# RWKV attention into a Sinkhorn mixture of experts on one core: attention scores in two diagonal blocks of 64 tokens with a half state, and three moves in the start phase

## The chip, the core and the metric

The kernel runs on one core of a Trainium2 chip. The core has five engines that run side by side, each through its own list of instructions in order: TensorE (PE, matmuls; its weight loads are listed as PEld), VectorE (DVE), ScalarE (ACT), GpSimd (POOL) and SyncE (SP, which here issues the DMAs). An engine waits for another through semaphores that stand in its instructions. The matmuls write PSUM, eight banks of accumulators that DVE and ACT can read. The metric is the device time of one execution in microseconds, given as the median of several runs.

## The reference

The first half is a linear attention with a decaying state, token by token; the second half routes every token through eight experts, with gates balanced by eight Sinkhorn rounds.

```python
for t in range(S):                       # B=4, H=8, S=768, D=48
    kt, vt, rt = (k[:, :, t], v[:, :, t], r[:, :, t])
    cur = np.einsum('bhd,bhe->bhde', u[None] * kt, vt)
    y[:, :, t] = np.einsum('bhd,bhde->bhe', rt, state + cur)
    state = w[None, :, :, None] * state + np.einsum('bhd,bhe->bhde', kt, vt)
...
x = y.transpose(0, 2, 1, 3).reshape(B * S, H * D)        # 3072 x 384
P = np.exp(logits - logits.max())                        # logits = x @ w_gate
for _ in range(8):
    P /= P.sum(1, keepdims=True) + 1e-09
    P /= P.sum(0, keepdims=True) + 1e-09
    P *= N / E
for e in range(E):                                       # E=8, F=1024
    out += P[:, e:e + 1] * (np.maximum(x @ w1[e], 0.0) @ w2[e])
```

## The kernel before

**Tokens.** The 3072 tokens are 24 tiles of 128 (`NTT`), six tiles to a batch (`NCHB`). The attention is computed in chunks of 128 tokens: r and k are multiplied with tables of powers of the decay, so that within a chunk the scores of a head are one masked product, and what earlier chunks left is a state matrix per head. Heads lie in pairs (`NPAIR` = 4), one head of a pair on partitions 0 to 63, the other on 64 to 127.

**The steps.** A Python loop over `i` from 0 to `NTT + 2` writes the program in a software pipeline; step `i` writes, in this order: the loads of a later tile on SP; `prep(i+2)` (r on POOL, k on DVE, tiles `rp` and `kp`); `bonus_dot(i+1)` (POOL); `stage_b(i+1)` (PE transposes into `prT`, `pkT`, ACT copies to `rT`, `kT`); `scale_x` and `low_x` of tile `i-2` (DVE and ACT, tile `xsc`, then a transposing DMA to `hbx`); one unit of expert work on PE; `stage_c(i)`; up to two units of expert work; `stage_d(i-1)` and `finish(i-1)` (DVE or ACT make `x`); small gate products (`px`). Nothing reorders it afterwards: each engine runs its part in the order written, and a tile framework puts in the semaphore waits that the uses of the tiles ask for.

**Scores and state.** `stage_c` (line 473) makes the scores `pA` of a tile in two PSUM tiles, one for each half of the head pairs' partitions, in 16 matmuls of 64 by 64 weights over 128 columns. Two masked copies on DVE (`copy_predicated`) take them to `at`. The product k by v of the chunk, `pu`, goes to a PSUM tile of its own in 8 matmuls over all 128 tokens, unless the tile is the last of its batch, and DVE adds it to the state `S`, which POOL then multiplies with the decay of a chunk (`wbd`). In a batch's first tile the DVE does that multiplication itself.

**Output.** `stage_d` (line 518) makes `py`: 8 matmuls of the state (`py<-S`; none in a batch's first tile) and 16 of the masked scores (`py<-vn,at`).

**PSUM.** `prT`, `pkT`, the two `pA`, `pu` and `py` take turns in four buffers (pool `ps3`); a tile that takes a buffer waits until the one before it there has been read.

**Expert work beside it.** Tile by tile the finished `x` feeds the first expert: units of 9 matmuls (`ph<-hbx,ws`, then `hb` on ACT and DVE) and of 12 (`po<-ws,hb`, then `stg`). In steps 2 to 9 a plan (`PLAN`, line 696) places the splitting of that expert's weights into two f16 parts: maxima (`am`, `bm`), their reduction on DVE (`ar`, `br`), over partitions by PE (`ax`, `bx`), scales, high parts on ACT, low parts on DVE (`al`, `bl`). From step 9 on, further steps of DVE, ACT and POOL that combine tokens for the later experts are placed at two points of each step (`prepare`; `ws<-hbx` and `xv<-ws,xv` in the trace).

**After the attention** (line 813 on) come the other seven experts in 14 half stages, dense matmuls.

Of the kernel before, what the change touches and what calls it, by code (L numbers as in the profile page):

```python
# [8 lines left out]
F32 = mybir.dt.float32  # L9
# [4 lines left out]
ALU = mybir.AluOpType  # L14
# [19 lines left out]
def rwkv_sinkhorn_moe(  # L34
# [30 lines left out]
    HP = 64  # L65
# [5 lines left out]
    NSUM = 4  # L71
# [222 lines left out]
    def spin(n):  # L294
        pz = ps2.tile([P, TB], F32, tag="po", name="pz")
        for _ in range(n):
            T.matmul(pz, zeros[:, :P], zeros, start=True, stop=True)


    loads = {}  # L300
    early_home = xv0.rearrange("p n l q -> p (n l q)")

    def load_part(tt, nm, src):
        b, c = divmod(tt, NCHB)
        if 3 <= tt <= 5 and nm != "v":
            t_ = part(early_home, F32, (2 * (tt - 3) + "rk".index(nm)) * H * D, (H, D))
        else:
            t_ = ld.tile([P, H, D], F32, tag=nm + "n", name=f"{nm}n_{tt}", bufs=5 if nm == "v" else 3)
        Q.dma_start(t_, src[b, :, c * C : (c + 1) * C, :].rearrange("h t d -> t h d"))
        loads.setdefault(tt, {})[nm] = t_  # L310
# [38 lines left out]
            unit[:, :1, 1:].broadcast_to([P, n // HP, HP]), 0.0,  # L349
        )  # L350

    spin(13)
    wbd = ac.tile([P, NPAIR, 2, D], F32, name="wbd")
    mask = ac.tile([P, C], F32, name="mask")
    maski = mask.bitcast(I32)

    rp_ = [ac.tile([P, H, HP], F32, name=f"rp{i}") for i in range(2)]
    kp_ = [ac.tile([P, H, HP], F32, name=f"kp{i}") for i in range(3)]
    at_ = [ac.tile([P, H, C], F32, name=f"at{i}") for i in range(2)]

    ss_ = [ac.tile([P, NPAIR, 2, D], F32, name=f"S{i}") for i in range(3)]
    for t_ in rp_[:1] + kp_[:1] + rp_[1:] + kp_[1:]:
        G.memset(t_[:, :, D:], 0.0)
    fill(at_[0].rearrange("p h c -> p (h c)"))
# [25 lines left out]
    for j in range(2):  # L390
        rows = slice(j * HP, j * HP + D)
# [3 lines left out]
    for src, dst in ((tab, rtab), (tabr, ktab)):  # L395
# [6 lines left out]
    S_.copy(ub.rearrange("p h d -> p (h d)"), pub[:, : H * D])  # L402

    G.memset(mask, 1.0)
    G.affine_select(
        out=mask, in_=mask, compare_op=ALU.is_gt, fill=0.0, base=0,
        pattern=[[1, C]], channel_multiplier=-1,
    )
    for t_ in ss_:
        for j in range(2):  # L410
            G.memset(t_[j * HP : (j + 1) * HP, :, 1 - j, :], 0.0)

# [23 lines left out]
    st = {}  # L436
# [4 lines left out]
    def prep(tt):  # L441
        ld_ = loads[tt]
        (G if tt else V).tensor_tensor(rp_[tt % 2][:, :, :D], ld_["r"], rt4, op=ALU.mult)
        V.tensor_tensor(kp_[tt % 3][:, :, :D], ld_["k"], kt4, op=ALU.mult)
        st[tt] = {}

    def bonus_dot(tt):
        ld_ = loads[tt]
        rk = at2.tile([P, H, D], F32, tag="rk", name=f"rk_{tt}", bufs=3)
        G.tensor_tensor(rk, ld_["r"], ld_["k"], op=ALU.mult)  # L450
        G.tensor_tensor(rk, rk, ub, op=ALU.mult)
        st[tt]["rk"] = rk

    def bonus(tt):
        vn = loads[tt]["v"]
# [6 lines left out]
    def stage_b(tt):  # L462
        d = st[tt]
        for nm, src in (("rT", rp_[tt % 2]), ("kT", kp_[tt % 3])):
            pt = ps3.tile([P, NPAIR, P], F32, tag="pa", name=f"p{nm}_{tt}")
            sv = src.rearrange("p (a j) d -> p a (j d)", j=2)
            for p_ in range(NPAIR):
                T.transpose(pt[:, p_, :], sv[:, p_, :], ident)
            dst = at2.tile([P, NPAIR, P], F32, tag=nm, name=f"{nm}_{tt}", bufs=3 if nm == "rT" else 2)
            S_.copy(dst, pt)  # L470
            d[nm] = dst

    def stage_c(tt, between):
        d = st[tt]
        c = tt % NCHB
        rT, kT = d["rT"], d["kT"]
        at = at_[tt % 2].rearrange("p (a g) c -> p g a c", g=2)
        pas = []
        for g in range(2):
            pa = ps3.tile([P, NPAIR, C], F32, tag="pa", name=f"pA_{tt}_{g}")  # L480
            pas.append(pa)
        for a in range(NPAIR):
            for g in range(2):
                rows = slice(g * HP, g * HP + HP)
                for hs in (slice(0, HP), slice(HP, C)):
                    T.matmul(pas[g][hs, a, :], kT[rows, a, hs], rT[rows, a, :], start=True, stop=True)
        between()
        for g in range(2):
            V.copy_predicated(
                at[:, g], maski.unsqueeze(1).broadcast_to([P, NPAIR, C]), pas[g]  # L490
            )
        if c < NCHB - 1:
            vn = loads[tt]["v"]
            kp = kp_[tt % 3].rearrange("p (a j) d -> p a (j d)", j=2)
# [9 lines left out]
            for j in range(2):  # L504
                rows = slice(j * HP, (j + 1) * HP)
                if c == 0:
                    V.tensor_tensor(sn[rows, :, j, :], pu[rows], wbd[rows, :, j, :], op=ALU.mult)
                else:
                    V.tensor_tensor(sn[rows, :, j, :], pu[rows], d["S"][rows, :, j, :], op=ALU.add)
            if c:  # L510
                for j in range(2):
                    rows = slice(j * HP, (j + 1) * HP)
                    G.tensor_tensor(
                        sn[rows, :, j, :], sn[rows, :, j, :], wbd[rows, :, j, :], op=ALU.mult
                    )
            st.setdefault(("S", tt + 1), sn)

    def stage_d(tt):
        d = st[tt]
        c = tt % NCHB  # L520
# [5 lines left out]
        halves = [slice(i * HP, (i + 1) * HP) for i in range(2)]  # L526
        first = True
        pyf = py.rearrange("p h d -> p (h d)")
        if c > 0:
            for p_ in range(NPAIR):  # L530
                for hs in halves:
                    T.matmul(
                        pyp[hs, p_, :], d["rT"][:, p_, hs], d["S"][:, p_].rearrange("p j d -> p (j d)"),
                        start=first, stop=False, skip_group_check=True,
                    )
                first = False
        for h in range(H):
            for hs in halves:
                T.matmul(
                    py[hs, h, :], at[:, h, hs], vn[:, h, :],  # L540
                    start=first, stop=(h == H - 1 and tt >= NSUM), skip_group_check=True,
                )
            first = False
        d["py"] = pyf

    def finish(tt):
# [144 lines left out]
    for sg in range(3):  # L691
# [15 lines left out]
    def planned(i, pos):  # L707
        for nm in PLAN.get(i, {}).get(pos, "").split():
            wsteps.pop(nm)()
# [3 lines left out]
        3: [(7, "v")],  # L713
    }

    def n_steps(i, j):
# [8 lines left out]
    bonus_dot(0)  # L725
    for i in range(NTT + 3):
        if i == 1:
            gate_max()
        if i + 2 < NTT:
            for tt, nms in LOADS.get(i, [(i + 4, "rkv")]):  # L730
                for nm in nms if tt < NTT else "":
                    load_part(tt, nm, {"r": r, "k": k, "v": v}[nm])
            if i:
                prep(i + 2)
        if i + 1 < NTT and i:
# [26 lines left out]
        if i in (2, 3, 5):  # L762
            low_x(i - 2)
        if i == 4:
            for c_ in (slice(0, FHC), slice(FHC, FC)):
                Q.dma_start(raws[1][:, c_], w2[0, c_.start * P : c_.stop * P].rearrange("(c p) d -> p c d", p=P))
        planned(i, "b")
        if i == 0:
            fill(at_[1].rearrange("p h c -> p (h c)"))
            stage_b(1)  # L770
            bonus_dot(1)
            bonus(0)
        elif 5 <= i <= NTT:
            work(2 if i > 8 else 1)
# [603 lines left out]
```

## Time and profile before

| what | value |
|---|---|
| median of 3 runs | 1525.42 us (1524.48 to 1527.28) |
| the profiled execution's own time | 1524.22 us |
| its span, first to last instruction | 1522.7 us |
| PE matmul busy | 1508.2 us, 10280 records |
| DVE, ACT, POOL busy | 1000.7, 685.0, 568.8 us |
| attention, steps 0 to 24 | about the first 220 us |

A row of the timeline gives the start and the length of a run of equal instructions in us, the engine, the line, the operation with the tile that it writes and those that it reads, the shapes, the count, and in brackets how long the engine stood idle before and who ended that. Every line number there is 30, the helper through which all engines are called, so the tile names tell the places. An f32 matmul of the program leaves two records, so the 16 matmuls of the scores are `x32`. The end of a matmul's record is modelled and lies some hundred ns behind the start of the next one's; steps on PE are best read from start to start.

### The profile page before, as it was taken

Reading aid. Unit: us, or ns where it says so; the run is one execution under the profiler, and the core shown is the slowest. Engines: PE = TensorE matmul, PEld = TensorE weight load, DVE = VectorE, ACT = ScalarE, POOL = GpSimd, SP = SyncE. Lnnn points to the kernel's source line nnn. Section 1 sums busy time; section 2 is a strip of 40 time slices with the busy share of each in tenths; the row PEclk is TensorE's granted clock in tenths of the full one; section 3 lists DMA queues with packets and bytes.
Section 4 is the critical chain, followed back from the end, with each engine's and each line's share of the span. In section 5 each row is a group of like instructions: output and inputs, shape, how many; then the busy total and the mean of one; then the engine's idle time right before and its main releaser. Section 6 shows DMA issues by size and latency. Waiting matters only on the chain.

```text
span 1522.7 us, 26106 instructions
## 1 busy us (share of the span) xinstructions
PE 1508.2 (99%) x10280; PEld 852.8 (56%) x10280; DVE 1000.7 (66%) x1658; ACT 685.0 (45%) x1261; POOL 568.8 (37%) x682
## 2 busy tenths in 40 slices
PE   8999999999999999999999999999999999999998
PEld 6677765555555555555555555555555555555555
DVE  8877758676566666666676666666565666566563
ACT  6544434444354544545454544544354444444320
POOL 8677956010214234242524234242424233242200
PEclk9999999999999999999999999999999999999999
DMA  9655523211345676666656676645455454555434
GB/s 194 137 122 108 104 64 103 84 40 58 102 83 75 91 130 87 120 87 123 94 75 123 91 130 88 118 62 94 61 88 64 60 99 58 97 61 94 57 94 131
DMA packets 186725, 142.97 MB, mean 94 GB/s; under 512 B 109538, under 2 KB 180836, under 8 KB 186596
## 3 DMA queue, kind: packets, MB, share of 16 engines
q0 software_dynamic: 44928, 61.36, 32.5%
q1 hardware_dynamic: 141458, 79.87, 19.7%
q8 instruction: 82, 1.34, 0.4%
q14 instruction: 47, 0.39, 0.1%
q10 hardware_dynamic: 210, 0.00, 0.0%
HBM read 55.20 MB, written 80.23 MB: 89 GB/s over the span
## 4 chain that ended last, share of the span: by engine, by line
PE 95%; DVE 3%; ACT 1%; issue 1%; DMA 0%; ACTq 0%; DVEq 0%
PE po L30 49%; PE bZ L30 12%; PE bY L30 12%; PE ph L30 5%; PE bA L30 5%; PE bB L30 5%; PE bC L30 2%; PE py L30 2%; PE pA L30 1%; PE pu L30 1%; PE prT L30 1%; PE pkT L30 1%; DVE hb L30 0%; DVE at L30 0%; PE pz L30 0%
## 5 line engine op out<-in xcount | busy, mean ns | idle before, releaser
L30 PE MATMUL po<-ws,hbx 128*128 128x384 f16 x3360 | 736.8, 326 | 0.0
L30 POOL DMA_DIRECT2D accd<-stg x288 | 249.7, 867 | 694.9 <-ACT stg L30 674.3
L30 PEld LDWEIGHTS <-hbx 128*128 128x128 f16 x3504 | 334.1, 98 | 293.1 <-issue 0.6
L30 PEld LDWEIGHTS <-ws 128*128 128x128 f16 x3096 | 301.6, 98 | 247.1 <-DMA hbx<-xsc 2.5
L30 ACT ACTIVATE hbx<-tb 128x512 f16<-128x512 f32 x224 | 141.1, 630 | 448.6 <-DVE tb L30 448.6
L30 PE MATMUL po<-ws,hb 128*128 128x384 f16 x1248 | 323.0, 326 | 0.5 <-DVE ws L30 0.5
L30 DVE TENSOR_TENSOR tb<-bY,tb 128x512 f32<-128x512 f32 x168 | 116.1, 691 | 195.7 <-PE bY L30 195.4
L30 ACT ACTIVATE stg<-po,pe 128x384 f32<-128x384 f32 x312 | 179.2, 574 | 122.4 <-PE po L30 96.8
L30 PE MATMUL bZ<-xv,ws 128*128 128x512 f16 x840 | 227.0, 379 | 0.5 <-DVE tb L30 0.5
L30 PE MATMUL bY<-xv,ws 128*128 128x512 f16 x840 | 227.0, 379 | 0.0
L30 DVE TENSOR_TENSOR tb<-bZ,tb 128x512 f32<-128x512 f32 x168 | 115.4, 687 | 135.3 <-PE bZ L30 135.3
L30 PEld LDWEIGHTS <-hb 128*128 128x128 f16 x1248 | 121.4, 98 | 93.9 <-issue 1.1
L30 POOL TENSOR_TENSOR ucb<-rawb 128x256 f32<-128x256 f32 x84 | 76.4, 960 | 116.8 <-DMA rawb<-in_moe_w_dram 116.8
L30 DVE TENSOR_TENSOR tb<-bB,tb 128x512 f32<-128x512 f32 x112 | 77.4, 691 | 49.0 <-PE bB L30 47.1
L30 PE MATMUL ph<-hbx,ws 128*128 128x384 f16 x576 | 104.3, 326 | 3.0 <-DMA hbx<-xsc 2.2
L30 DVE SCALAR_TENSOR_TENSOR hb<-tb,hbx 128x512 f16<-128x512 f32 x112 | 77.2, 689 | 24.7 <-ACT hbx L30 19.5
L30 PE MATMUL bA<-xv,ws 128*128 128x512 f16 x336 | 90.8, 379 | 0.0
L30 PE MATMUL bB<-xv,ws 128*128 128x512 f16 x336 | 90.8, 379 | 0.0
L30 DVE SCALAR_TENSOR_TENSOR hbx<-tb,hbx 128x512 f16<-128x512 f32 x112 | 77.4, 691 | 14.7 <-ACT hbx L30 10.4
L30 ACT COPY tb<-bZ 128x512 f32<-128x512 f32 x56 | 32.7, 585 | 65.6 <-PE bZ L30 65.5
L30 DVE SCALAR_TENSOR_TENSOR hb<-ph,hb 128x384 f16<-128x384 f32 x64 | 35.3, 552 | 26.9 <-ACT hb L30 26.2
L30 DVE TENSOR_REDUCE wms<-rawb 128x1 f32<-128x768 f32 x56 | 51.7, 943 | 0.0
(173 smaller groups left out, 1471.5 us busy)
## 6 DMA issues: line engine op xcount, KB each, us to landing
accd<-stg POOLq DMA_DIRECT2D x288, 192.0 KB, 3.7
rawb<-in_moe_w_dram SPq DMA_DIRECT2D x28, 768.0 KB, 7.5
e0d<-stg SPq DMA_DIRECT2D x48, 192.0 KB, 2.1
hb<-e0d SPq DMA_DIRECT2D x48, 192.0 KB, 3.6
vn<-in_v_dram SPq DMA_DIRECT2D x24, 192.0 KB, 2.9
accd<-stg SPq DMA_DIRECT2D x24, 192.0 KB, 1.8
accd<-hb POOLq DMA_DIRECT2D x24, 192.0 KB, 4.7
rawb<-accd SPq DMA_DIRECT2D x24, 192.0 KB, 2.5
```

Source lines behind the costliest of these rows:

```text
L30: return lambda *a, **k: self.tc.keep_in_program_order(f(*a, **k))
```

## The change

Within a tile of 128 tokens only the two diagonal blocks of 64 by 64 scores are now computed as scores. What the first 64 tokens give to the last 64 goes through a half state `Sh`, the state after 64 tokens.

- `pA` has 64 columns in place of 128 for each head, `at` and the mask likewise; the matmuls are as many as before and half as wide, the masked copies half as large.
- The product k by v is made for each half by itself, on 64 tokens: 16 matmuls in place of 8, and 8 in a batch's last tile, which had none. It has no PSUM tile of its own any more: it is written into the columns of the two `pA` tiles behind the scores.
- DVE makes `Sh` of the state and the first half's product (two adds; two copies in a batch's first tile), and the new state of `Sh` and the second half's product. POOL's two multiplications by the decay now come in a batch's first tile too.
- `stage_d` multiplies the first 64 tokens of a tile with `S` and the last 64 with `Sh` (in a batch's first tile the last 64 alone), and each diagonal block of `at` with its own 64 rows of v.
- Start: 10 in place of 13 idle matmuls (`spin`); POOL makes r times k of tiles 0 and 1 ahead of its other work.
- Step 4: tile 2's transposing DMA is issued ahead of the loads of tile 8 and of w2, not behind them.
- Step 7: the reduction `br` of w2's maxima goes ahead of the low part `al3` on DVE.

```diff
-    spin(13)
+    spin(10)
-    at_ = [ac.tile([P, H, C], F32, name=f"at{i}") for i in range(2)]
+    at_ = [ac.tile([P, H, HP], F32, name=f"at{i}") for i in range(2)]
+    sh_ = [ac.tile([P, NPAIR, 2, D], F32, name=f"Sh{i}") for i in range(2)]
...
     def stage_c(tt, between):
-        pas = []
-        for g in range(2):
-            pa = ps3.tile([P, NPAIR, C], F32, tag="pa", name=f"pA_{tt}_{g}")
-            pas.append(pa)
+        banks = [ps3.tile([P, NPAIR * (HP + D)], F32, tag="pa", name=f"pA_{tt}_{g}") for g in range(2)]
+        pas = [b_[:, : NPAIR * HP].rearrange("p (a c) -> p a c", c=HP) for b_ in banks]
+        pus = [b_[:, NPAIR * HP :].rearrange("p (a d) -> p a d", d=D) for b_ in banks]
         for a in range(NPAIR):
-            for g in range(2):
-                rows = slice(g * HP, g * HP + HP)
-                for hs in (slice(0, HP), slice(HP, C)):
-                    T.matmul(pas[g][hs, a, :], kT[rows, a, hs], rT[rows, a, :], start=True, stop=True)
+            for g, rows in enumerate(halves):
+                for hs in halves:
+                    T.matmul(pas[g][hs, a, :], kT[rows, a, hs], rT[rows, a, hs], start=True, stop=True)
         between()
         for g in range(2):
             V.copy_predicated(
-                at[:, g], maski.unsqueeze(1).broadcast_to([P, NPAIR, C]), pas[g]
+                at[:, g], maski.unsqueeze(1).broadcast_to([P, NPAIR, HP]), pas[g]
             )
-        if c < NCHB - 1:
-            pu = ps3.tile([P, NPAIR, D], F32, tag="pa", name=f"pu_{tt}")
-            for p_ in range(NPAIR):
-                for j in range(2):
+        last_ = c == NCHB - 1
+        for p_ in range(NPAIR):
+            for j, rows in enumerate(halves):
+                for h_ in range(1 if last_ else 2):
                     T.matmul(
-                        pu[j * HP : (j + 1) * HP, p_, :], kp[:, p_, j * HP : (j + 1) * HP],
-                        vn[:, 2 * p_ + j, :], start=True, stop=True,
+                        pus[h_][rows, p_, :], kp[halves[h_], p_, rows], vn[halves[h_], 2 * p_ + j, :],
+                        start=True, stop=True,
                     )
+        d["Sh"] = sh = sh_[tt % 2]
+        for j, rows in enumerate(halves):
+            if c == 0:
+                V.tensor_copy(sh[rows, :, j, :], pus[0][rows])
+            else:
+                V.tensor_tensor(sh[rows, :, j, :], pus[0][rows], d["S"][rows, :, j, :], op=ALU.add)
+        if not last_:
             sn = ss_[tt % 3]
...
+            for j, rows in enumerate(halves):
+                V.tensor_tensor(sn[rows, :, j, :], pus[1][rows], sh[rows, :, j, :], op=ALU.add)
...
     def stage_d(tt):
+        begun = set()
+        for p_ in range(NPAIR):
+            for i_, hs in enumerate(halves):
+                src = d["Sh"] if i_ else d.get("S")
+                if src is None:
+                    continue
+                T.matmul(
+                    pyp[hs, p_, :], d["rT"][:, p_, hs], src[:, p_].rearrange("p j d -> p (j d)"),
+                    start=i_ not in begun, stop=False, skip_group_check=True,
+                )
+                begun.add(i_)
         for h in range(H):
-            for hs in halves:
+            for i_, hs in enumerate(halves):
                 T.matmul(
-                    py[hs, h, :], at[:, h, hs], vn[:, h, :],
+                    py[hs, h, :], at[hs, h, :], vn[hs, h, :],
...
-        7: {"b": "al3 bm3", "d": "br"},
+        7: {"b": "bm3 br al3"},
...
+    dot(0)
+    dot(1)
     prep(0)
+    dot_u(0)
...
         if i == 4:
+            load_round(i, "rk")
             for c_ in (slice(0, FHC), slice(FHC, FC)):
                 Q.dma_start(raws[1][:, c_], w2[0, c_.start * P : c_.stop * P].rearrange("(c p) d -> p c d", p=P))
+            load_round(i, "v")
```

On PE, the end of the scores of tile 9 and the product k by v behind them, with the semaphores that an instruction waits for. A name such as `DVE_49` is the counter of that engine's finished instructions, `DMAHW1_49` that of a DMA queue; `vn` is v, `kp` the prepared k. Before:

```order
L30 MATMUL pA_9_0_1297<-rT_9_1117,kT_9_1124 64x128 x2
L30 MATMUL pA_9_1_1298<-rT_9_1117,kT_9_1124 64x128 x2
L30 MATMUL pA_9_0_1297<-rT_9_1117,kT_9_1124 64x128 x2
L30 MATMUL pA_9_1_1298<-rT_9_1117,kT_9_1124 64x128 x2
L30 MATMUL pu_9_1317<-vn_9_729,kp0_159 64x48 [waits DMAHW1_49,Activation_49]
L30 MATMUL pu_9_1317<-vn_9_729,kp0_159 64x48 x7
```

The same place in the changed kernel:

```order
L30 MATMUL pA_9_0_1395<-rT_9_1206,kT_9_1213 64x64 x2
L30 MATMUL pA_9_1_1396<-rT_9_1206,kT_9_1213 64x64 x2
L30 MATMUL pA_9_0_1395<-vn_9_784,kp0_156 64x48 [waits DMAHW1_49,DVE_49]
L30 MATMUL pA_9_1_1396<-vn_9_784,kp0_156 64x48 [waits DVE_49]
L30 MATMUL pA_9_0_1395<-vn_9_784,kp0_156 64x48
L30 MATMUL pA_9_1_1396<-vn_9_784,kp0_156 64x48
L30 MATMUL pA_9_0_1395<-vn_9_784,kp0_156 64x48
```

The product is written to the tiles of the scores, and its first matmul into each of the two tiles waits for an instruction of DVE, where before it waited for v's load and for ACT.

On DVE, the masked copies of tile 9 and what stands around them. Before:

```order
L30 TENSOR_REDUCE dg_9_1294<-rk_9_1109 128x8 [waits Pool_49]
L30 COPY_PREDICATED at1_163<-mask_156,pA_9_0_1297 128x4x128 [waits PE_49]
L30 COPY_PREDICATED at1_163<-mask_156,pA_9_1_1298 128x4x128 [waits PE_49]
L30 TENSOR_TENSOR S0_164<-pu_9_1317,S2_166 64x4x48 [waits PE_49,Pool_49]
L30 TENSOR_TENSOR S0_164<-pu_9_1317,S2_166 64x4x48 [waits Pool_49]
```

The same place in the changed kernel:

```order
L30 TENSOR_REDUCE dg_9_1392<-rk_9_1198 128x8 [waits Pool_49]
L30 COPY_PREDICATED at1_160<-mask_153,pA_9_0_1395 128x4x64 [waits PE_49]
L30 COPY_PREDICATED at1_160<-mask_153,pA_9_1_1396 128x4x64 [waits PE_49]
L30 TENSOR_TENSOR Sh1_165<-pA_9_0_1395,S2_163 64x4x48 [waits PE_49,Pool_49]
L30 TENSOR_TENSOR Sh1_165<-pA_9_0_1395,S2_163 64x4x48 [waits Pool_49]
L30 TENSOR_TENSOR S0_161<-pA_9_1_1396,Sh1_165 64x4x48 [waits DVE_49,PE_49]
L30 TENSOR_TENSOR S0_161<-pA_9_1_1396,Sh1_165 64x4x48 [waits DVE_49]
```

The copies keep their place in DVE's list and are half as wide; two adds for the half state stand between them and the adds of the state.

More of the change, by code (lines that the diff above doesn't have):

```diff
@@ L350, in fill @@
         )
-    spin(13)
+    spin(10)
     wbd = ac.tile([P, NPAIR, 2, D], F32, name="wbd")
-    mask = ac.tile([P, C], F32, name="mask")
+    mask = ac.tile([P, HP], F32, name="mask")
     maski = mask.bitcast(I32)
@@ L404, in rwkv_sinkhorn_moe @@
     G.memset(mask, 1.0)
[L405 to L409, printed above, removed]
+    for j in range(2):
+        m_ = mask[j * HP : (j + 1) * HP]
+        G.affine_select(
+            out=m_, in_=m_, compare_op=ALU.is_gt, fill=0.0, base=0,
+            pattern=[[1, HP]], channel_multiplier=-1,
+        )
+    for t_ in ss_ + sh_:
         for j in range(2):
@@ L444, in prep, with dot @@
         V.tensor_tensor(kp_[tt % 3][:, :, :D], ld_["k"], kt4, op=ALU.mult)
-        st[tt] = {}
-    def bonus_dot(tt):
+    def dot(tt):
         ld_ = loads[tt]
@@ L450, in bonus_dot, with dot_u @@
         G.tensor_tensor(rk, ld_["r"], ld_["k"], op=ALU.mult)
+        st[tt] = {"rk": rk}
+    def dot_u(tt):
+        rk = st[tt]["rk"]
         G.tensor_tensor(rk, rk, ub, op=ALU.mult)
-        st[tt]["rk"] = rk
+    def bonus_dot(tt):
+        dot(tt)
+        dot_u(tt)
     def bonus(tt):
@@ L471, in stage_b @@
             d[nm] = dst
+    halves = [slice(i * HP, (i + 1) * HP) for i in range(2)]
     def stage_c(tt, between):
@@ L489, in stage_c @@
             V.copy_predicated(
-                at[:, g], maski.unsqueeze(1).broadcast_to([P, NPAIR, C]), pas[g]
+                at[:, g], maski.unsqueeze(1).broadcast_to([P, NPAIR, HP]), pas[g]
             )
-        if c < NCHB - 1:
-            vn = loads[tt]["v"]
-            kp = kp_[tt % 3].rearrange("p (a j) d -> p a (j d)", j=2)
-            pu = ps3.tile([P, NPAIR, D], F32, tag="pa", name=f"pu_{tt}")
-            for p_ in range(NPAIR):
-                for j in range(2):
+        vn = loads[tt]["v"]
@@ L499, in stage_c @@
+        kp = kp_[tt % 3].rearrange("p (a j) d -> p a (j d)", j=2)
+        last_ = c == NCHB - 1
+        for p_ in range(NPAIR):
+            for j, rows in enumerate(halves):
+                for h_ in range(1 if last_ else 2):
                     T.matmul(
-                        pu[j * HP : (j + 1) * HP, p_, :], kp[:, p_, j * HP : (j + 1) * HP],
-                        vn[:, 2 * p_ + j, :], start=True, stop=True,
-                    )
-            sn = ss_[tt % 3]
[L504 to L515, printed above, removed]
+                        pus[h_][rows, p_, :], kp[halves[h_], p_, rows], vn[halves[h_], 2 * p_ + j, :],
+                        start=True, stop=True,
+                    )
+        d["Sh"] = sh = sh_[tt % 2]
[4 more added lines that the diff above has]
+                V.tensor_tensor(sh[rows, :, j, :], pus[0][rows], d["S"][rows, :, j, :], op=ALU.add)
@@ L516, in stage_c @@
+        if not last_:
+            sn = ss_[tt % 3]
+            for j, rows in enumerate(halves):
+                V.tensor_tensor(sn[rows, :, j, :], pus[1][rows], sh[rows, :, j, :], op=ALU.add)
+            for j, rows in enumerate(halves):
+                G.tensor_tensor(
+                    sn[rows, :, j, :], sn[rows, :, j, :], wbd[rows, :, j, :], op=ALU.mult
+                )
             st.setdefault(("S", tt + 1), sn)
@@ L519, in stage_d @@
         d = st[tt]
-        c = tt % NCHB
         vn = loads[tt]["v"]
@@ L524, in stage_d @@
         pyp = py.rearrange("p (a j) d -> p a (j d)", j=2)
-        halves = [slice(i * HP, (i + 1) * HP) for i in range(2)]
-        first = True
         pyf = py.rearrange("p h d -> p (h d)")
-        if c > 0:
-            for p_ in range(NPAIR):
-                for hs in halves:
[L532 to L536, printed above, removed]
+        begun = set()
[7 more added lines that the diff above has]
+                    start=i_ not in begun, stop=False, skip_group_check=True,
+                )
+                begun.add(i_)
         for h in range(H):
-            for hs in halves:
+            for i_, hs in enumerate(halves):
                 T.matmul(
-                    py[hs, h, :], at[:, h, hs], vn[:, h, :],
-                    start=first, stop=(h == H - 1 and tt >= NSUM), skip_group_check=True,
+                    py[hs, h, :], at[hs, h, :], vn[hs, h, :],
+                    start=i_ not in begun, stop=(h == H - 1 and tt >= NSUM), skip_group_check=True,
                 )
-            first = False
+                begun.add(i_)
         d["py"] = pyf
@@ L714, in rwkv_sinkhorn_moe, with load_round @@
     }
+    def load_round(i, of="rkv"):
+        for tt, nms in LOADS.get(i, [(i + 4, "rkv")]):
+            for nm in nms if tt < NTT else "":
+                if nm in of:
+                    load_part(tt, nm, {"r": r, "k": k, "v": v}[nm])
     def n_steps(i, j):
@@ L724, in rwkv_sinkhorn_moe @@
     prep(2)
-    bonus_dot(0)
     for i in range(NTT + 3):
@@ L729, in rwkv_sinkhorn_moe @@
         if i + 2 < NTT:
-            for tt, nms in LOADS.get(i, [(i + 4, "rkv")]):
-                for nm in nms if tt < NTT else "":
-                    load_part(tt, nm, {"r": r, "k": k, "v": v}[nm])
+            if i != 4:
+                load_round(i)
             if i:
@@ L770, in rwkv_sinkhorn_moe @@
             stage_b(1)
-            bonus_dot(1)
+            dot_u(1)
             bonus(0)
```

## Prediction

> **What bounds the kernel now.** I began with the page's first and fourth parts, busy times and the chain of work that ended last.
>
> ```profile
> PE 1508.2 (99%) x10280; PEld 852.8 (56%) x10280; DVE 1000.7 (66%) x1658; ACT 685.0 (45%) x1261; POOL 568.8 (37%) x682
> PE 95%; DVE 3%; ACT 1%; issue 1%; DMA 0%; ACTq 0%; DVEq 0%
> ```
>
> TensorE is the bound: it has work in 99% of the span, and 95% of the chain lies on it. So an edit counts by what it does to PE's own time and by any wait that it puts in front of PE. Next the windows over the attention (columns: busy us and instructions of each engine).
>
> ```profile
> 100.00:150.00 50.00, 50.00 (x713) 35.98 (x713) 37.96 (x73) 21.09 (x49) 37.34 (x42) 1.00 0.55 114
> ```
>
> PE has no gap at all in these five steps; DVE and POOL are busy 38 and 37 of 50 us. They are not the bound, but they are far from idle. Then the timeline of PE through one step (step 16, tile 16).
>
> ```profile
> 138.41 0.60 PE L30 MATMUL pkT<-ident,kp 128*128 128x128 f32 x4
> 138.84 1.63 PE L30 MATMUL ph<-hbx,ws 128*128 128x384 f16 x9
> 140.40 1.10 PE L30 MATMUL pA<-rT,kT 64*64 64x128 f32 x32
> 141.44 0.67 PE L30 MATMUL pu<-vn,kp 128*64 128x48 f32 x16
> 142.04 2.12 PE L30 MATMUL po<-ws,hb 128*128 128x384 f16 x12
> 144.00 1.63 PE L30 MATMUL ph<-hbx,ws 128*128 128x384 f16 x9
> 145.56 0.88 PE L30 MATMUL py<-S,rT 128*64 128x96 f32 x16
> 146.27 1.09 PE L30 MATMUL py<-vn,at 128*64 128x48 f32 x32
> 147.29 0.31 PE L30 MATMUL px<-wgp,hbx 128*128 128x16 f16 x6
> ```
>
> From start to start: the scores take 1.04 us, the product k by v follows at once with 0.60, the state's share of py 0.71, the scores' share 1.02. And DVE over the same stretch:
>
> ```profile
> 138.79 0.55 DVE L30 TENSOR_TENSOR x<-py,rk 128x384 f32<-128x384 f32 x1
> 139.26 2.62 DVE L30 TENSOR_TENSOR ws<-hbx 128x768 f32<-128x768 f16 x2
> 141.80 1.35 DVE L30 TENSOR_TENSOR kp<-kn,ktab 128x384 f32<-128x384 f32 x1
> ...
> 144.29 0.62 DVE L30 SCALAR_TENSOR_TENSOR xsc<-x,xs,xsc 128x384 f16<-128x384 f32 x1 [0.68 <-ACT xsc L30]
> 144.83 0.55 DVE L30 SCALAR_TENSOR_TENSOR hb<-ph,hb 128x384 f16<-128x384 f32 x1
> 145.29 0.54 DVE L30 TENSOR_REDUCE dg<-rk 128x8 f32<-128x384 f32 x1
> 145.75 1.36 DVE L30 COPY_PREDICATED at<-mask,pA 128x512 f32<-128x512 int32 x2
> 146.99 0.73 DVE L30 TENSOR_TENSOR S<-pu,S 64x192 f32<-64x192 f32 x2
> 148.23 1.25 DVE L30 TENSOR_TENSOR ws<-hbx 128x768 f32<-128x768 f16 x1
> 149.40 0.54 DVE L30 TENSOR_TENSOR x<-py,rk 128x384 f32<-128x384 f32 x1
> ```
>
> The point to see: the scores of tile 16 are done at 141.50, but DVE ends their masked copies only at 147.11, 5.61 us later. Before the change nobody minds: `at` is read a step later, and PE goes straight on to `pu`.
>
> **The wait that the change adds.** The product k by v is now written into the tiles of the scores, and by the order rows its first matmul into each waits for DVE. The only DVE instruction that uses such a tile between the scores and the product is its masked copy. PE takes its matmuls in order, so behind this wait stand the product, two units of expert work, both parts of `py`, and the next step; and DVE's list up to the next copies begins with `x`, which waits for that `py`. What was slack becomes a loop: PE's `py`, DVE's and ACT's work up to the copies, PE's product.
>
> So the first term is, for each of the 24 tiles, the time from the end of the scores to the end of the copies. I read it in the same way for all; first, shortest regular and last tile:
>
> ```profile
> 11.65 1.10 PE L30 MATMUL pA<-rT,kT 64*64 64x128 f32 x32 [0.24 <-ACT kT L30]
> 12.86 1.37 DVE L30 COPY_PREDICATED at<-mask,pA 128x512 f32<-128x512 int32 x2
> 130.89 1.10 PE L30 MATMUL pA<-rT,kT 64*64 64x128 f32 x32
> 132.39 1.34 DVE L30 COPY_PREDICATED at<-mask,pA 128x512 f32<-128x512 int32 x2
> 205.87 1.10 PE L30 MATMUL pA<-rT,kT 64*64 64x128 f32 x32
> 208.28 1.34 DVE L30 COPY_PREDICATED at<-mask,pA 128x512 f32<-128x512 int32 x2
> ```
>
> That is 1.48, 1.74 and 2.65 us. The nine tiles 0 to 8 sum to 19.9 us (1.5, 1.5, 0.8, 2.2, 3.1, 1.8, 2.9, 3.2, 3.0), the fifteen tiles 9 to 23 to 51.8 (2.7, 4.8, 2.8, 4.9, 2.6, 2.9, 1.7, 5.6, 4.6, 4.8, 2.6, 3.8, 2.0, 3.3, 2.7): 71.6 together.
>
> Corrections of each tile: the product started 0.06 before the scores' record ended (141.44 against 141.50), plus 0.06. A release costs 0.05, as DVE's end at 62.81 and PE's start at 62.86 show below. The copies have half the elements: a pair of 512 takes 1.36, a pair of 192 (the adds to S) 0.73; on a straight line a pair of 256 takes 0.86, so minus 0.50. The bounds are 0.73 and 1.36. Together minus 0.39 a tile, minus 9.4: **62.2 us**.
>
> **The change's other parts.** *Scores:* 32 records of half the width; between `pu`'s pace (0.60 for eight rounds of 64-column weights) and no change, so up to 0.44 us less a tile. I take 0.44 and count it at nothing: PE only reaches the wait earlier. Without the wait it would be 10.6 us.
>
> *Product:* 32 records on 64 rows in place of 16 on 128. If four lie side by side, as the scores' four 64 by 64 quarters do (32 records in 1.04), it stays 0.60; in pairs it would be 1.2, 12 us over the 20 tiles that had it. The scores' row is the nearest, so 0. The four last tiles of a batch had none: plus 4 times 0.60, 2.4; they wait for the first copy alone, minus 4 times 0.43, 1.7.
>
> *State into py:* in the four first tiles of a batch one half of the array now works, where none did. Both halves side by side took 0.71, so one alone does too: plus 2.8. Elsewhere the count is the same.
>
> *Scores into py:* the same pairs with half the rows; I leave 1.02 as it is. Half of it would be 12 us less, twice 24 more.
>
> The Trainium skill speaks against this part: "TensorEngine Tiling (Array Packing)", Gotcha 1, says that row tiles write different PSUM banks and cannot use one bank at the same time, and the two diagonal blocks lie on different rows and go to one `py`. No run shows that form yet; the old `py` used two column halves of one bank side by side.
>
> *DVE:* 0.73 more for `Sh`, and it now stands about 0.8 while PE makes the product. Both lie behind the copies, beside 5.9 us in which PE does the product, expert work and py (141.44 to 147.29): 0.8, twice 0.73, a 0.55 and a 1.25 make 4.1. Were that cover gone, `x` would come later and each tile lose the difference. One tile gains: `x` at 149.40 came 2.1 behind py's end at 147.29 since DVE was behind; with PE waiting that backlog goes, minus 1.1.
>
> *POOL:* two products more in four tiles, beside 13 idle us in 50; r times k early fills idle time at the start: 0.
>
> **Start phase.** These are PE's waits there.
>
> ```profile
> 1.52 5.73 PE L30 MATMUL pz<-xv 128*128 128x512 f16 x13 [1.52 <-DVE xv L30]
> 10.82 0.59 PE L30 MATMUL pz<-xv 128*128 128x512 f16 x2
> 39.58 1.64 PE L30 MATMUL ph<-hbx,ws 128*128 128x384 f16 x9 [2.22 <-DMA hbx<-xsc]
> 62.66 0.15 DVE L30 TENSOR_REDUCE wma<-wm 128x1 f32<-128x4 f32 x1
> 62.86 0.27 PE L30 MATMUL pmax_w<-ident,wma 128*1 128x128 f32 x1 [1.68 <-DVE wma L30]
> 72.70 0.97 PE L30 MATMUL po<-ws,hb 128*128 128x384 f16 x5 [0.54 <-DVE ws L30]
> ```
>
> Three idle matmuls less: 3 times 0.44, minus 1.3 if the tables are ready, else 0. The moves of the transfer and of `br` are aimed at the waits of 2.22 and 1.68; since PE comes 7 us later at the first (the delays of tiles 0 to 4), both and the 0.54 go anyway: minus 4.4. What is late next is the copies.
>
> **Sum.** 62.2 - 1.7 + 2.4 + 2.8 - 1.1 - 1.3 - 4.4 = 58.9 us on the profiled execution's 1524.22, so 1583.1; the median of the runs is 1.20 above that execution, so **1584**. The dense stage behind the attention is PE's own and moves along.
>
> **Rivals.**
>
> *DVE catches up (0.12).* With PE slower, the tasks between `x` and the copies (the two `ws` of 1.3 each above) would run in pauses. Then tiles 6 to 23 would each lose what tile 15 does, 1.74 - 0.39 = 1.35: 24.3, tiles 0 to 5 10.8 - 2.3 = 8.5, the other terms -2.2 (no backlog left): +30.6, 1556. For it: the pauses exist. Against it: DVE's order is fixed, and the `ws` stand behind `x`, which waits for py.
>
> *PE's clock falls (0.10).* The first 13 idle matmuls start 0.44 apart, the later two about half that: PE began at half speed until about 7 us, losing some 2.8 us of work. Five tiles (10, 12, 16, 17, 18) would keep PE idle for over 4 us; if each brought such a fall, 14 us more: 1598. Against it: after the 2.22 us gap nine `ph` took 1.64 as elsewhere. The Trainium skill, "TensorE: Matmul & The Clock Gate", Part 1, has half speed follow an idle window of about 3.4 us; by that rule these five are exposed where the 2.22 was not.
>
> *The diagonal blocks take turns (0.03).* If two row halves cannot write `py` at once, 1.02 becomes 2.04: 24 us more, 1608.
>
> *The other side: the wait is covered (0.05).* If the copies were over whenever PE reaches the product, the rest would stand: -10.6 + 2.4 + 2.8 - 1.3, and some 2.9 of the waits of 2.22 and 1.68 gone by the moves: -9.6, 1516. It decides at copies ending about when the scores do. Against it: the smallest of the 24 intervals is 0.8 us and all others at least 1.46, and half-sized copies take 0.5 off. It is also the case in which the instruction waited for is an earlier one of DVE than the copy.
>
> **How the numbers follow.** The forecast has 0.70, with 1570 to 1595 as its own range (copies 0.73 to 1.36, a tile 0.1 to 0.5 either way). To hold eight in ten the range reaches to the first two rivals: 1556 to 1602. Faster by over 0.2% (3 us, about what a measurement of this kernel can tell from no change) has 0.05, within 0.01, slower 0.94.
>
> **What would show it.** In the changed profile PE's first product matmul (now under `pA<-vn,kp`) starts 0.05 after the second masked copy ends, in every tile, with idle time put down to DVE `at`, over 50 us in all; a step takes about 12 us in place of 9.5; scores take 0.6. A clock fall shows as `ph` taking over 3 us for nine. Wrong would be a product that starts before its copies end, or copies that follow the scores within a microsecond.

## The result, and the profile after

| what | before | after |
|---|---|---|
| median of 5 runs each | 1525.42 us (1524.48 to 1527.28) | 1596.34 us (1592.23 to 1599.75) |
| ratio | 1 | 1.0465 (95% interval 1.0453 to 1.0476) |
| the profiled execution's own time | 1524.22 us | 1598.36 us |
| its span | 1522.7 us | 1596.9 us |
| PE busy in it | 1508.2 us | 1536.6 us |
| PE idle in it (span less busy) | 14.5 us | 60.3 us |

The changed kernel is 70.9 us slower. Forecast were 1584 and a range of 1556 to 1602. Of the 74.2 us that the span grew, 45.8 are idle time of PE and 28.4 are busy time. So there are two things to find, a wait and something that made PE's own work longer.

The first is in the waits of PE (us in total, times, longest):

```profile
PE pA L30 <- DVE at L30: 49.9, 24, 5.0
PE pz L30 <- DVE xv L30: 1.5, 1, 1.5
PE ph L30 <- DVE hb L30: 0.8, 1, 0.8
PE prT L30 <- DVE rp L30: 0.8, 1, 0.8
```

One wait in each of the 24 tiles, for the masked copy `at`, and nothing else of size; the old waits of 2.22 (`hbx`) and 1.68 (`wma`) are gone. The second shows in two groups of the expert's matmuls (us busy, mean ns of one; then the idle time ahead of them), which have the same count and shape as before. Before:

```profile
L30 PE MATMUL po<-ws,hb 128*128 128x384 f16 x1248 | 323.0, 326 | 0.5 <-DVE ws L30 0.5
L30 PE MATMUL ph<-hbx,ws 128*128 128x384 f16 x576 | 104.3, 326 | 3.0 <-DMA hbx<-xsc 2.2 <-DVE hb L30 0.8
```

After:

```profile
L30 PE MATMUL po<-ws,hb 128*128 128x384 f16 x1248 | 332.9, 336 | 0.0
L30 PE MATMUL ph<-hbx,ws 128*128 128x384 f16 x576 | 114.1, 347 | 0.8 <-DVE hb L30 0.8
L30 PE MATMUL pA<-vn,kp 64*64 64x48 f32 x704 | 24.2, 239 | 50.2 <-DVE at L30 49.9
```

The same matmuls take 19.7 us longer in these two groups; the third line is the product with its idle time. The timeline of PE around tile 16 shows both things together:

```profile
181.34 1.63 PE L30 MATMUL ph<-hbx,ws 128*128 128x384 f16 x9
182.89 0.69 PE L30 MATMUL pA<-rT,kT 64*64 64x64 f32 x32
188.57 1.44 PE L30 MATMUL pA<-vn,kp 64*64 64x48 f32 x32 [4.98 <-DVE at L30]
189.94 4.02 PE L30 MATMUL po<-ws,hb 128*128 128x384 f16 x12
193.76 1.97 PE L30 MATMUL ph<-hbx,ws 128*128 128x384 f16 x9
```

PE stands still for 4.98 us, and then twelve `po` take 4.02 us; before, and in other steps, 2.11 or 2.12. DVE in that time:

```profile
181.13 0.55 DVE L30 TENSOR_TENSOR x<-py,rk 128x384 f32<-128x384 f32 x1
181.60 2.62 DVE L30 TENSOR_TENSOR ws<-hbx 128x768 f32<-128x768 f16 x2
184.15 1.34 DVE L30 TENSOR_TENSOR kp<-kn,ktab 128x384 f32<-128x384 f32 x1
...
186.62 0.62 DVE L30 SCALAR_TENSOR_TENSOR xsc<-x,xs,xsc 128x384 f16<-128x384 f32 x1 [0.68 <-ACT xsc L30]
187.16 0.55 DVE L30 SCALAR_TENSOR_TENSOR hb<-ph,hb 128x384 f16<-128x384 f32 x1
187.63 0.54 DVE L30 TENSOR_REDUCE dg<-rk 128x8 f32<-128x384 f32 x1
188.09 0.76 DVE L30 COPY_PREDICATED at<-mask,pA 128x256 f32<-128x256 int32 x2
```

This is the loop that was forecast: the `x` that ends the step before, seven microseconds of DVE and ACT work, the copies, and only then PE's product. PE starts 0.05 after the *first* copy ends (188.57 against 188.52), not after the second (188.85).

The granted clock goes with the slow `po`. The clock's rows in the trace change only on a grid of 3.41 us; these are windows on that grid (length; busy us and count of PE, PEld, DVE, ACT, POOL; granted clock of PE; DMA share and GB/s):

```profile
170.55:173.96 3.41, 1.91 (x53) 1.32 (x46) 2.32 (x6) 0.56 (x2) 1.08 (x2) 1.00 0.63 120
173.96:177.37 3.41, 3.41 (x13) 1.63 (x11) 1.42 (x4) 0.49 (x1) 2.16 (x3) 0.50 0.01 2
177.37:180.78 3.41, 3.41 (x64) 2.65 (x63) 0.79 (x1) 1.42 (x2) 0.00 (x0) 1.00 0.00 0
180.78:184.20 3.42, 2.81 (x48) 1.89 (x46) 3.42 (x5) 1.74 (x5) 2.36 (x2) 1.00 0.99 129
184.20:187.61 3.41, 0.00 (x0) 0.00 (x0) 2.66 (x7) 0.99 (x2) 0.88 (x1) 1.00 0.89 227
187.61:191.02 3.41, 2.45 (x36) 1.80 (x37) 2.08 (x7) 0.00 (x0) 0.83 (x1) 0.50 0.00 0
191.02:194.44 3.42, 3.42 (x13) 1.57 (x12) 0.58 (x2) 0.40 (x1) 1.17 (x2) 0.50 0.00 0
```

A window in which PE is idle for 3.41 us is followed by two at half speed, and one with only 1.50 us idle (3.41 less 1.91) by one. In the changed kernel 16 such windows (54.6 us) run at half speed between the start and the last three microseconds, before the change none after 7.2 us. PE is idle for 4.8 of these 54.6 us. Counted from start to start, its work in the other 49.8 us takes 23.0 us longer than the same instructions take at full speed: 19.3 for `ph` and `po`, 1.7 for the product, 2.0 for parts of `py`. That is most of the 28.4 us of busy time.

The chain of work that ended last, first place to look before the change, helps little here:

```profile
PE 81%; DVE 2%; ACT 0%; issue 0%; ACTq 0%; DVEq 0%
```

The shares make only 83% of the span: the chain is not followed back into the attention (it has no piece between 180 and 200 us), so the loop has to be read from waits and timeline.

### The profile page after: what moved, and what is told of

It reads as the page before. It is cut to its first block, busy times and chain, and to the rows that moved or that the text cites. A ratio compares the mean times of both kernels' runs of the same rounds, so it can differ in the third digit from the quotient of the medians.

```text
span 1596.9 us, 27035 instructions
## 1 busy us (share of the span) xinstructions
PE 1536.6 (96%) x10693; PEld 864.6 (54%) x10693; DVE 1000.1 (63%) x1706; ACT 683.9 (43%) x1261; POOL 569.8 (36%) x695
## 3 DMA queue, kind: packets, MB, share of 16 engines
q0 software_dynamic: 44928, 61.36, 30.7%
## 4 chain that ended last, share of the span: by engine, by line
PE 81%; DVE 2%; ACT 0%; issue 0%; ACTq 0%; DVEq 0%
PE po L30 44%; PE bZ L30 11%; PE bY L30 11%; PE bA L30 5%; PE bB L30 4%; PE ph L30 2%; PE bC L30 2%; PE py L30 0%; DVE xv L30 0%; DVE wms L30 0%; DVE hb L30 0%; DVE tb L30 0%; DVE rs_s L30 0%; DVE pm L30 0%; DVE ws L30 0%
## 5 line engine op out<-in xcount | busy, mean ns | idle before, releaser
L30 PE MATMUL po<-ws,hb 128*128 128x384 f16 x1248 | 332.9, 336 | 0.0
L30 PEld LDWEIGHTS <-hb 128*128 128x128 f16 x1248 | 124.8, 101 | 99.6 <-issue 10.1
L30 PE MATMUL ph<-hbx,ws 128*128 128x384 f16 x576 | 114.1, 347 | 0.8 <-DVE hb L30 0.8
L30 DVE SCALAR_TENSOR_TENSOR hb<-tb,hbx 128x512 f16<-128x512 f32 x112 | 77.2, 689 | 24.6 <-ACT hbx L30 19.5
L30 DVE SCALAR_TENSOR_TENSOR hb<-ph,hb 128x384 f16<-128x384 f32 x64 | 35.4, 554 | 60.5 <-ACT hb L30 60.3
L30 PE MATMUL pA<-vn,kp 64*64 64x48 f32 x704 | 24.2, 239 | 50.2 <-DVE at L30 49.9
L30 ACT ACTIVATE hb<-ph 128x384 f16<-128x384 f32 x64 | 31.2, 488 | 79.7 <-PE ph L30 79.2
```

Of the source, the lines that this page charges most:

```text
L30: return lambda *a, **k: self.tc.keep_in_program_order(f(*a, **k))
```

## The experiments

Each ran beside the kernel before on the same chip. Medians of before lay at 1526.5 to 1527.0 there; ratios are to these.

### 1. The product ahead of the scores

```diff
         pus = [b_[:, NPAIR * HP :].rearrange("p (a d) -> p a d", d=D) for b_ in banks]
-        for a in range(NPAIR):
-            for g, rows in enumerate(halves):
-                for hs in halves:
-                    T.matmul(pas[g][hs, a, :], kT[rows, a, hs], rT[rows, a, hs], start=True, stop=True)
-        between()
...
         vn = loads[tt]["v"]
...
                         start=True, stop=True,
                     )
+        for a in range(NPAIR):
+            for g, rows in enumerate(halves):
+                for hs in halves:
+                    T.matmul(pas[g][hs, a, :], kT[rows, a, hs], rT[rows, a, hs], start=True, stop=True)
+        between()
...
```

The scores and the masked copies move to behind the product, whose matmuls stand between the two places.

> The product k by v is written ahead of the scores in each step, into the same columns of the same tiles; everything else is the changed kernel. If the wait for the masked copies is the cause of the loss, no product matmul waits for DVE at any more (49.9 us in 24 waits go), PE's clock stays at full speed through the attention, and the scores' halved width counts: 24 x 0.44 = 10.6 less, the added products and state matmuls 2.4 + 2.8 more, so 1510 to 1522 us, faster than the kernel before. If instead the block form itself is slow (its matmuls on 64 rows, the half state's adds on DVE), the time stays above 1560.

Measured: 1525.6 us (1523.15 to 1526.67), ratio 0.999 (0.9981 to 0.9999). All 24 waits for `at` are gone, and one window alone runs at half speed behind the start. So order decides, by 70 us. The hoped gain did not come. In the start phase PE waits for DVE more than before; DVE carries the splitting of the weights there and now the adds for `Sh`, but that these adds are the reason is not shown:

```profile
PE ph L30 <- DVE hb L30: 3.3, 3, 1.3
PE pmax_w L30 <- DVE inv_s L30: 1.6, 1, 1.6
...
PE ph L30 <- DVE ws L30: 1.1, 2, 0.8
PE prT L30 <- DVE rp L30: 1.0, 1, 1.0
```

From step 9 on it gains little: from the transposes of tile 10 to those of tile 23 (13 steps) 122.7 us, before 124.4. The scores take 5.3 us less over these steps, but the state's part of `py` 2.7 more and the scores' part 0.5 more.

### 2. The moves alone

The kernel before with the shorter `spin`, `r` times `k` ahead, and the edits of steps 4 and 7; the scores in the old form.

```diff
-    spin(13)
+    spin(10)
...
-        7: {"b": "al3 bm3", "d": "br"},
+        7: {"b": "bm3 br al3"},
...
+    dot(0)
+    dot(1)
     prep(0)
+    dot_u(0)
...
         if i == 4:
+            load_round(i, "rk")
             for c_ in (slice(0, FHC), slice(FHC, FC)):
...
```

> The kernel before with the moves of the start alone (10 idle matmuls, r times k early, tile 2's transfer ahead of loads and w2, br ahead of al3). The waits of 2.22 us for the transfer and of 1.68 for the reduction shrink, the start comes about 1 us sooner: 1520 to 1524 us. If the moves only shift the waits, 1525, no change; if they cost something themselves (the loads of tile 8 late), above 1527.

Measured: 1523.55 us (1523.22 to 1525.2), ratio 0.998 (0.9971 to 0.9989): 3 us faster. The wait for `hbx` fell from 2.2 to 1.2 us and that for `wma` from 1.7 to 0.2, with 1.2 for `inv_s` in the second's place. Others grew: 1.7 for `wc` at the start, which was not there, and 2.7 in place of 0.8 for `hb`.

### 3. The block form alone, product behind the scores

The changed kernel with these moves undone.

```diff
-    spin(10)
+    spin(13)
...
-        7: {"b": "bm3 br al3"},
+        7: {"b": "al3 bm3", "d": "br"},
...
-    dot(0)
-    dot(1)
...
-            load_round(i, "rk")
...
```

> The changed kernel with the moves of the start undone, so the block form alone. If the wait and the clock make the loss, it stays: 1594 to 1602 us, with 24 waits for at of about 50 us. If the moves are the cause (late loads, POOL's early work), it returns to near 1525.

Measured: 1600.0 us (1598.63 to 1606.52), ratio 1.0492 (1.0471 to 1.0513); PE waits 50.7 us for `at` in 24 waits, and 2.5 us for tile 2's transfer (`hbx`). The whole loss is the block form's, and the moves give back 3 to 4 us here too.

### 4. The scores three times over

A filler that changes nothing but PE's work ahead of the wait: 64 records more a tile, 0.96 us, 23 us in all.

```diff
-        for a in range(NPAIR):
...
+        for _ in range(3):
+            for a in range(NPAIR):
+                for g, rows in enumerate(halves):
...
```

> The changed kernel with each score matmul made three times over (the same values, written again), about 0.95 us more PE work in each of the 24 tiles, 23 us in all, ahead of the wait. If the wait sets the pace, this work is free where the copies come more than 1 us after the scores: the wait falls from 49.9 to about 27 us and the time stays within 5 us of 1596, or falls by some 5 to 15 us if the added work keeps PE's clock up, of which the trace shows 55 us at half speed now. If PE's own work were the bound, 1596 + 23 = 1619.

Measured: 1586.24 us (1585.14 to 1590.67), ratio 1.0387 (1.0371 to 1.0403): **10 us faster than the changed kernel, with 23 us more work on PE**. The wait fell from 49.9 to 30.4 us and the half-speed time behind the start from 54.6 to 30.7. The span agrees. 23.0 more work, 19.5 less wait and 23.9 us less at half speed make -8.5 if time at half speed costs half its length, and -6.6 if it costs 23.0 in 54.6 as in the changed kernel; measured 1589.1 - 1596.9 = -7.8. Around tile 15 the changed kernel had

```profile
172.25 1.00 PE L30 MATMUL pA<-vn,kp 64*64 64x48 f32 x32 [1.48 <-DVE at L30]
173.19 2.35 PE L30 MATMUL ph<-hbx,ws 128*128 128x384 f16 x9
175.34 3.12 PE L30 MATMUL po<-ws,hb 128*128 128x384 f16 x12
```

and this kernel has

```profile
170.42 1.63 PE L30 MATMUL pA<-rT,kT 64*64 64x64 f32 x96
172.61 1.00 PE L30 MATMUL pA<-vn,kp 64*64 64x48 f32 x32 [0.56 <-DVE at L30]
173.54 1.64 PE L30 MATMUL ph<-hbx,ws 128*128 128x384 f16 x9
175.01 2.11 PE L30 MATMUL po<-ws,hb 128*128 128x384 f16 x12
```

the same work at full speed. The clock is a cost of the wait, beside the wait.

### 5. The product first, without the moves

Experiments 1 and 3 in one kernel: the product stands ahead of the scores, and the moves are undone.

```diff
-    spin(10)
+    spin(13)
...
-        for a in range(NPAIR):
...
         vn = loads[tt]["v"]
...
+        for a in range(NPAIR):
...
```

> The changed kernel with the product k by v ahead of the scores, as in the first experiment, and with the start phase and steps 4 and 7 as before the change: the block form without its wait, and nothing else. If the two parts simply add up, the moves are worth what they gave alone (1523.55 against 1527.0, some 3 us), so this one stands at 1526 to 1531. Rival: the moves cost the block form something in steps 5 to 9, where it lost 2.8 us by step 9; then this one is at 1519 to 1524.

Measured: 1528.84 us (1527.87 to 1530.04), ratio 1.0015 (1.0006 to 1.0024). The block form without its wait is at best no gain: 0.15% slower than before. PE waits 4.4 us for `hbx` and 2.3 for `wma` here, more than before the change (2.2 and 1.7). With the moves (experiment 1) it was 1525.6, so these are worth 3 us in either form, and the rival, that they cost the block form something, falls.

### 6. The scores five times over

```diff
-        for a in range(NPAIR):
...
+        for _ in range(5):
+            for a in range(NPAIR):
...
```

> The changed kernel with the 16 matmuls of the scores written five times: 4 times 0.48 us of further PE work in each of 24 tiles, 46 us, ahead of the wait for the masked copies. Theory: half of the loss beyond the wait is the PE clock, which this work keeps up. The wait falls from 49.9 to 12 to 18 us, the half-speed stretches from 55 us to under 16, the time is 1579 to 1587, still below the changed kernel's 1596. Rival: the slower expert matmuls have another cause than PE's pauses; then the half-speed time stays at 40 us or more and the time is 1600 to 1610.

Measured: 1611.93 us (1610.81 to 1614.26), ratio 1.0563 (1.0547 to 1.0579). A miss. The wait fell to 18.7 us, a little over its range, but the half-speed time stayed at 30.7 us, and PE had a new kind of pause:

```profile
PE pA L30 <- DVE at L30: 18.7, 24, 3.1
PE pA L30 <- issue: 8.8, 6, 2.9
```

Four of the six stops (7.7 us) lie in the middle of a tile's 160 score records, two (1.1 us) ahead of the product; PE waits there for nothing that the profile names. Against experiment 4 that makes 23.0 more work, 8.8 more pauses and 11.7 less wait, +20.1; the span grew by 22.3 (1611.4 less 1589.1). So the filler is no further proof of the clock; why the stops appear was not followed up.

### 7. Old form to tile 8, block form with the product first from tile 9

The kernel of experiment 2, with two forms of `stage_c` and `stage_d`. Behind tile 8 POOL turns the mask into that of the blocks and clears `at`, whose free half holds `Sh`.

```diff
     def stage_c(tt, between):
+        if tt >= 9:
+            return block_c(tt, between)
...
     def stage_d(tt):
+        if tt >= 9:
+            return block_d(tt)
```

> Before with the moves; tiles 0 to 8 in the old form, tiles 9 to 23 in the block form with the product ahead of the scores. Theory: the block form gains some 0.35 us a step where PE is the bound (steps 9 to 23 of the first experiment) and loses where DVE is (steps 5 to 9). Then this kernel is 15 times 0.35 = 5 us below the moves alone: 1517 to 1520. Rival: the gain per step was PE catching up on what it had lost earlier; then it is 1522 to 1525, no better than the moves alone.

Measured: 1521.37 us (1520.79 to 1523.57), ratio 0.9969 (0.9957 to 0.9982). That is 0.3% below the kernel before and the lowest of all. Against the moves alone (0.998, measured on another chip) the intervals overlap, and the trace says why: the 13 steps from the transposes of tile 10 on take 122.1 us against 124.4 with the moves alone, 0.18 us a step and not 0.35. It lies between what the two theories expected.

### 8. The product behind the second expert work

```diff
-            stage_c(i, between)
+            pus_ = stage_c(i, between)
...
             work(2 if i > 8 else 1)
+        if i < NTT:
+            stage_c2(i, pus_)
```

`stage_c` ends with the masked copies here; `stage_c2` has the product, the adds for `Sh` and the state.

> The changed kernel with the product k by v, and the adds behind it, written behind the second expert work of the step in place of directly behind the scores; it still waits for the masked copies. Theory: the wait costs only because nothing stood between the scores and the product; with 3.7 us of expert work there (from step 9 on; 1.6 to 2.1 in steps 5 to 8, none before) nearly all of the 49.9 us go: under 12 us are left, the clock stays up, and the time is 1524 to 1534. Rival: the loop through py, x and DVE holds whatever stands in between; the wait then stays above 25 us and the time above 1550.

Measured: 1542.69 us (1539.84 to 1543.51), ratio 1.0105 (1.0089 to 1.012). 9 waits of together 12.3 us are left (24 of 49.9 in the changed kernel), and four windows at half speed. The rival falls, and the theory was too hopeful by 9 us: in tiles 10 and 16 the first copy ended 5.9 and 5.3 us behind the scores, more than the 3.7 us of expert work (4.3 us of wait), and in steps 1 to 4 no expert work stood between (6.1 us).

### 9. The product at its place, in PSUM tiles of its own

This takes away what the product waits for and leaves every PE instruction where it is.

```diff
-        banks = [ps3.tile([P, NPAIR * (HP + D)], F32, tag="pa", name=f"pA_{tt}_{g}") for g in range(2)]
-        pas = [b_[:, : NPAIR * HP].rearrange("p (a c) -> p a c", c=HP) for b_ in banks]
-        pus = [b_[:, NPAIR * HP :].rearrange("p (a d) -> p a d", d=D) for b_ in banks]
+        pas = [ps3.tile([P, NPAIR, HP], F32, tag="pa", name=f"pA_{tt}_{g}") for g in range(2)]
...
+        pus = [ps3.tile([P, NPAIR, D], F32, tag="pa", name=f"pu_{tt}_{h_}") for h_ in range(1 if last_ else 2)]
```

> The changed kernel with the product k by v at its place directly behind the scores, but in two PSUM tiles of its own instead of the columns behind the scores. Theory: the product needs nothing of the masked copies; what it waits for is only the PSUM tile that it shares with them. Then all 24 waits for the copies go with the order of the instructions unchanged, and the time is that of the product placed first (1525.6): 1522 to 1530. Rival: seven PSUM tiles a step (six before the change) take turns in four buffers, and the copies or x hold the next one up; then PE waits over 8 us for ACT or DVE at prT, pkT, pA or py, and the time is 1533 to 1560.

Measured: 1527.03 us (1525.65 to 1527.63), ratio 1.0 (0.9991 to 1.0009). The product follows the scores at once, as before the change:

```profile
140.01 1.63 PE L30 MATMUL ph<-hbx,ws 128*128 128x384 f16 x9
141.57 0.69 PE L30 MATMUL pA<-rT,kT 64*64 64x64 f32 x32
142.08 0.83 PE L30 MATMUL pu<-vn,kp 64*64 64x48 f32 x32
```

No window between 7.4 us and the last two microseconds runs at half speed. In place of 49.9 us PE waits 4.8 us for copies, now with `py`, which takes the buffer of a score tile:

```profile
PE py L30 <- DVE at L30: 4.8, 8, 1.3
PE ph L30 <- DVE hb L30: 2.1, 3, 1.0
```

So the 70 us are the price of one shared PSUM tile: the columns of product and scores are apart, and the product needs nothing of the copies. Whether PE could safely write such a tile while DVE reads it, no run tests.

## Why the prediction was right, and where it was off

**The bound and the mechanism: right.** "What was slack becomes a loop" is what the trace shows, in all 24 tiles, and experiments 1 and 9 remove it by order alone and by tile alone. The one detail that was wrong is the release: the first pair of product matmuls waits for the first copy alone, 0.33 us before the second.

**The size: 1584 against 1596, by errors that partly cancel.** The measured terms are from the profiled executions, from start to start of PE's instructions. The first two count work at full speed, and what half speed adds stands in the fourth.

| term | forecast | measured |
|---|---|---|
| wait, with scores and product | 62.2 - 1.7 + 2.4 = 62.9 | 49.9 - 9.2 + 9.4 = 50.1 |
| other PE work of `py` | 2.8 | 6.3 |
| vanished waits, backlog, idle matmuls | -6.8 | -5.4 |
| PE's clock | 0 | 23.0 |
| sum | 58.9 | 74.0 (the time grew by 74.1) |

So the nearness of 1584 is in part luck: the mechanism was right, one term came out 13 us too large and another of 23 was not in the sum.

*Wait.* The scores' own time falls from 25.8 to 16.6 us in 24 tiles, which is the 9.2. The prediction counted that "at nothing: PE only reaches the wait earlier". That step failed: the time from the scores' end to the copies' end did not grow by it. Over the 24 tiles it fell from 71.6 to 57.2, the 12.0 that the smaller copies were to bring and 2.4 for copies of 0.76 in place of 0.86 per pair. The traces show that DVE's side of the loop became shorter, beyond the copies. From the end of a `py` to the next but one tile's scores PE takes as long as before in 17 of the 22 tiles that have such a `py` ahead. But `x` starts sooner behind that `py`, by 9.5 us over the 22 tiles and by 0.8 to 2.1 in eight of them, and from `x` to the copies 6.8 us less passes. Ahead of tile 17's copies stands now

```profile
196.47 1.14 PE L30 MATMUL py<-vn,at 64*64 64x48 f32 x32
197.65 0.56 DVE L30 TENSOR_TENSOR x<-py,rk 128x384 f32<-128x384 f32 x1
```

where `x` began 2.04 us behind the end of `py` before the change (149.40 against 147.36). The prediction took DVE's backlog off for this one tile alone, at 1.1 us; it stood in others too. So the rival "DVE catches up" came true in its effect, by some 0.4 us a tile and not the 1.35 that it named, and not in its way: in 19 of the 22 tiles DVE runs the same instructions between `x` and the copies as before. Some of them are shorter now (`xsc` takes 13.3 us in place of 16.0 in all there); why is not shown. The product (9.4) takes 0.94 from start to start (172.25 to 173.19 in tile 15) in place of 0.50 to 0.64 in 20 tiles, since its first pair starts 0.33 early and then waits inside the group; 0.6 in each of the four last tiles was new, as forecast.

*Clock.* This was a rival with 0.10, and it came true beside the likeliest case, not in its place. It counted "five tiles" whose wait would be "over 4 us", 14 us; the runs show two such waits (4.3 in tile 10, 4.98 in tile 16), but 16 windows and 23 us, because the fall needs far less than 4 us. The Trainium skill, "TensorE: Matmul & The Clock Gate", Part 1, which the prediction cites there, has an idle window of about 3.4 us as the trigger. The grid of 3.41 us agrees with it, the trigger does not: 1.50 us idle in one window (tile 15) was enough, as shown above.

*Other work of `py`.* One half of the array alone takes 0.8 us in the four first tiles (2.8 forecast, 3.2 measured). In the other 20 the state's part went from 0.71 to 0.81, and in all 24 the scores' part from 1.02 to 1.06, 2.1 and 1.0 us that the prediction left out.

**The rivals that did not come.** The diagonal blocks did not take turns: 32 records of `py<-vn,at` start within 0.92 us, against 0.87 before; the prediction had priced turns at double. So writing one `py` from two row halves with different partitions cost 0.05 us a tile here; the rule of the Trainium skill's "TensorEngine Tiling (Array Packing)", Gotcha 1, did not apply to this form. Nor was the wait covered; how it looks when it is, experiment 1 shows (1525.6): the forecast 1516 of that case was 10 us too low. It priced the halved scores at 0.44 us a tile, and they gave 0.41 a step from tile 10 on, but the longer `py` that the sum left out took most of it back (122.7 against 124.4, 0.13 a step), and PE waited more for DVE in the start phase.

**Start phase.** The moves are worth 3 us with the old form and with the block form, close to the 2.9 of the prediction's last rival. In the changed kernel the waits that they aim at are gone (`hbx` from 2.2 to nothing), but not for the prediction's reason. It held that they "go anyway", since PE comes later at the first. In experiment 3, without the moves, PE comes there 13 us later than before the change and still waits 2.5 us for `hbx`:

```profile
52.66 1.64 PE L30 MATMUL ph<-hbx,ws 128*128 128x384 f16 x9 [2.49 <-DMA hbx<-xsc]
```

So that wait went by the moves, most likely that of the transfer, and only the one for `wma` goes without them. Experiment 3 puts the moves at 3.7 us in the changed kernel, in runs that spread by more than that.

## What to carry to other kernels

Before giving a result a place in a PSUM tile that another engine still reads, look at what stands between the two on the in-order engine: data that are apart still wait when the tile is one, and here writing the product first or in tiles of its own, at no cost in instructions, was worth 70 us. When such a wait is priced from the trace before the change, the backlog that the other engine has there has to come off: it goes once PE waits (9.5 us here, of which the prediction took off 1.1). A wait of the bounding engine costs more than its length: the first microseconds behind it may run at half speed, so a pause of 1.5 us can cost twice that. And rivals are not exclusive: where one case brings a wait, price the other mechanisms that this wait sets off inside it.

## What the runs showed of the hardware

**The clock follows the share of PE's idle time in windows, not a whole idle window.** I divided the eleven profiles of this study into the 3.41 us windows of the clock's rows and took those between 8 and 300 us with full clock. Of those with under 1 us idle, 2 of 790 were followed by half speed; with 1.0 to 1.4 us, 1 of 31; with 1.4 to 1.7 us, 5 of 22; with 1.7 to 2.1 us, 12 of 14; with more, 16 of 16. The border lies near half a window, and idle time alone does not decide close to it. So by this count a pause is cheaper when it is split by the grid, and the grid's place is not the kernel's to choose: the first row at full clock began between 4.3 and 7.4 us in the eleven profiles.

**Small matmuls.** With 64 by 64 weights in f32, scores over 64 columns start 32 records within 0.48 us (before, over 128 columns, 0.84), and the product over 48 columns within 0.79 behind the wait and within 0.46 when it leads (experiment 1; 0.51 from start to start). Half the columns bring 0.53 of 1.04 us from start to start where the product follows at once (experiment 9). With 160 such records in a row PE stops at times for up to 2.9 us with no cause in the profile (experiment 6).
